# Batch 1's second product as half products in a fused attention and mixer kernel

## The chip, the cores and the metric

The kernel runs on one core of a Trainium2 chip. A core has a matrix engine (TensorE, "PE" in the profile; its weight loads are shown apart as "PEld"), a vector engine (VectorE, "DVE"), an activation engine (ScalarE, "ACT"), a general engine (GpSimd, "POOL") and an engine that mostly issues transfers (SyncE, "SP"). Each works through its own queue of instructions in order, and they meet through semaphores. TensorE's results go to PSUM, eight banks of 512 float32 columns in 128 partitions; a bank that holds a result can be written anew only when another engine has read the result out of it (here called evicting it). The metric is the device time of one execution in microseconds (us), as the median of some runs.

## The reference

Two steps, in float32, on 8 batches of 576 rows.

```python
# attention: q, k, v (8 batches, 8 heads, 576 rows, 64)
phi(x) = concat(relu(x) * cos_w, relu(x) * sin_w)          # 64 -> 128 features
kv  = einsum('bhsf,bhsd->bhfd', phi(k), v);  z = sum_s phi(k)
x   = einsum('bhsf,bhfd->bhsd', phi(q), kv) / (einsum('bhsf,bhf->bhs', phi(q), z) + 1e-6)
# mixer, on x as (8, 576, 512): U (576, 32), V (32, 576), w_ch1 (512, 2048), w_ch2 (2048, 512)
u   = x + (x^T U V)^T
out = u + relu(u @ w_ch1) @ w_ch2
```

Nearly all the arithmetic is in the last line: a *first product* of 512 by 2048 and a *second product* of 2048 by 512 for every row.

## The kernel before

**Rows and tiles.** Of a batch's 576 rows, 512 are four chunks of 128 rows (c = 0 to 3), and 64 are a tail; two batches' tails make one more chunk of 128 (pair pr = 0 to 3). The weights lie in SBUF as bf16 (`w1_bf`, `w2_bf`). Per batch b:

- attention: `q_prep` and `k_prep` (L307 to L327) make the features q_p and k_p from staged float32 loads (qst, kst), 128x512 at a time, on VectorE (L303) or ScalarE (L301); `v_prep` casts v (L130 is the helper that casts on VectorE or GpSimd, L128 the one on ScalarE); SyncE transposes q_p by transfer into q_pT (`qtr_dma`, L386); `kv_unit` (L334) makes kv on TensorE; `x_unit` (L410) and `x_two` (L1151) make x on TensorE, and VectorE normalises it (L407, L408, L427, L1178).
- u: `A_unit` (L447) and `u_mm` (L463) are the low-rank step on TensorE; `u_add` (L476, four a batch) adds x on VectorE into u_bf; `utr_dma` (L510) has SyncE transpose u_bf by transfer into uT, in two halves. `u_tail` (L483) does the same for a pair's tails.
- first product: `g1_main` (L561), 16 units (j) of four 512-column matmuls into a bank of tag "g"; ScalarE evicts each with relu into hid (L580). `g1_tail` (L596) is the same for a pair's tails.
- second product, whole: `g2_part` (L620), for each chunk four parts of four 512-column matmuls, and one eviction on VectorE that adds u (L653) and one store.
- second product, as seven half products: `half_part` (L743). The two chunks n and n + 2 and the two halves of w_ch2 in each direction are the 2x2 blocks of a block product with seven products instead of eight (sums of blocks before, sums of results after). Each half product is eight 256-column matmuls (L772). It needs sums of hid (`hid_sum` L704: four for each n, 128x1024 in bf16 on VectorE, the third and fourth in place) and sums of w_ch2 (`w2_sum` L682: eight halves, 128x1024 in bf16 on VectorE, made once). In the form "with g" the half products alternate with the units of the next batch's first product, in two banks. In the form "alone" they follow each other in three banks, ScalarE copies four of seven results out (L128), VectorE three, and GpSimd makes two additions of 128x512 float32 (L730).

**Order.** It is written out by hand: `slots` is a list of units of TensorE work, recorded one after the other, and `todo` holds what is recorded behind slot n. So every engine's queue is the order in which the slots and what is put behind them are recorded. `PLAN` (L871) gives each batch b its place w, and `attention_plan` (L880) puts the batch's attention at fixed distances from w: for b > 3 q from w - 20 or w - 24, k from w - 13 or w - 14, the transposes of q at w - 12 or w - 14 and on, kv at w and w + 2, x from w + 4, A at w + 14, u_mm at w + 16, the u_adds and their transposes from there; for b = 3 A is at w + 12 and u_mm at w + 14. The last entry of a PLAN row places the loads of the next batch's q, k and v. The slots before the change are:

| slots | unit |
|---|---|
| 0 to 15 | first product of batch 0, with batch 1's attention beside it |
| 16 to 31 | second product of batch 0, four chunks, whole |
| 32 to 47 | first product of batch 1 |
| 48 to 51 | first product of pair 0's tails |
| 52 to 55 | second product of the tails (cc = 4), whole |
| 56 to 71 | second product of batch 1 (cc = 5 to 8), whole |
| 72 to 87 | first product of batch 2 |
| 88 on | for b = 3 to 7: the first product of b, alternating with half products of b - 1 ("with g"), and pair tails |
| last | half products of batch 7 ("alone") and of the last two tails |

Batch 2's attention runs beside slots 30 to 64 (w = 46), batch 3's beside slots 52 to 86 (w = 64). The sums of w_ch2 stand behind slots 56 to 70. Pair 0's stores for chunks 1 to 3 and the tail wait in `late` until slot 92, those of cc = 5 and 6 until slot 65.

**Banks.** `Banks` (L57) hands out banks round robin by tag: g0, g1, g2 for "g", o0 and o1 for "o", two more for "X" and one for "T". `ring` and `turn` (L719) are the list that half products take their banks from.

Of the kernel before, what the change touches and what calls it, by code (L numbers as in the profile page):

```python
# [17 lines left out]
def kernel(  # L18
# [55 lines left out]
    ps = Banks()  # L74
# [543 lines left out]
    late = {}  # L618

    def g2_part(pr, cc, part):  # L620
# [48 lines left out]
            )  # L669

        if pr == 0 and 0 < cc < 7:
            late.setdefault(92 if cc < 5 else 65, []).append(store)
            return
        store()

# [6 lines left out]
    def w2_sum(n, half):  # L682

        a, b = (
            (W2[1], W2[0]), (W2[3], w2_s[0]), (W2[3], W2[1]), (W2[2], w2_s[1])
        )[n]
        js = slice(4 * half, 4 * half + 4)
        V_.tensor_tensor(
            out=w2_s[n][:, js], in0=a[:, js], in1=b[:, js], op=ALU.subtract
        )  # L690
# [169 lines left out]
    ORD = (4, 0, 1, 2, 3)  # L860

    def spare(at):
        if at < 72:
            return ("o", 2) if 32 <= at < 52 else ("g", 3)
        return ("o", 2) if at < 88 else ("s", 1)

    QORD = (4, 0, 1, 2, 3)  # L870
    PLAN = {  # L871
        2: (46, -15, V_, V_, -10, (-5, -4, -4)),
        3: (64, -12, V_, A_, -7, (3, 3, 18)),
        4: (100, (-20, 1, V_, V_), (-13, 2, A_, V_), -12, (-9, -4, -4)),
        5: (127, (-24, 2, A_, A_), (-14, 2, A_, V_), -14, (-8, -4, -4)),
        6: (157, (-24, 2, A_, A_), (-14, 2, A_, V_), -14, (-8, -4, -4)),
        7: (191, (-24, 2, A_, A_), (-14, 2, A_, V_), -14, ()),
    }

    def attention_plan(b):  # L880
# [47 lines left out]


        def two(at):  # L930
            return [T1, ("s", 1)] if at >= 88 else [spare(at)] * 2

        plan.append((w + a_at + 2, lambda: u_mm(b, *two(w + a_at + 2))))
        for j in range(4):
# [49 lines left out]
    T1 = ("T", 1)  # L984
# [219 lines left out]
    def put(at, thunk):  # L1204
        todo.setdefault(at, []).append(thunk)

    def sums(b, n, ats):
        for i, at in enumerate(ats):
            put(at, lambda i=i: hid_sum(b, n, i + 1))
# [4 lines left out]
    def tail_out(pr):  # L1214
        slots.extend(lambda p=p: g2_part(pr, 4, p) for p in range(4))
# [6 lines left out]
    slots += [lambda cc=cc, p=p: g2_part(0, cc, p) for cc, p in early]  # L1222
    slots += [g1(1, j) for j in range(NJ)]
    tail_slots(0)
    slots += [lambda cc=cc, p=p: g2_part(0, cc, p) for cc in range(4, 9) for p in range(4)]
    slots += [g1(2, j) for j in range(NJ)]
    put(len(slots) - 1, lambda: ps.give("g", ("g0", "g1")))
    alone = len(slots)
# [34 lines left out]
    put(at - 2, lambda: tail_store(nc.sync, 3, o_last(1), slice(0, 512)))  # L1263
    put(at - 1, lambda: tail_store(A_, 2, o_last(0), slice(256, 512)))
    for n in range(8):
        put((56, 58, 60, 62, 66, 67, 69, 70)[n], lambda n=n: w2_sum(n // 2, n % 2))
    for j, ts_ in beside.items():
        todo[j] = list(ts_) + todo.get(j, [])

# [10 lines left out]
    for b in range(2, B):  # L1280
        for at, t in attention_plan(b):
            put(at, t)
    for n in (65, 92):
        put(n, lambda n=n: [store() for store in late[n]])
    for i, s in enumerate(slots):
        s()
        for t in todo.get(i, []):
# [31 lines left out]
```

## Time and profile before

| what | value |
|---|---|
| median of 3 runs | 297.0 us (296.45 to 297.48) |
| the profiled execution | 296.4 us, span 294.6 us, granted TensorE clock 1.0 |
| TensorE (PE) busy | 286.1 us, 97% |
| VectorE (DVE) busy | 192.6 us, 65% |
| ScalarE (ACT) busy | 154.7 us, 53% |
| GpSimd (POOL) busy | 51.1 us, 17% |
| one first-product unit, four 512-column matmuls | 0.86 us on the chain |
| one half product, eight 256-column matmuls | 0.87 us on the chain |

The span is the time from the first to the last instruction of the program. In a timeline line the columns are the start and the time taken (us), engine, source line, operation, output tile <- input tiles, shapes and count; in brackets stands the idle time of the engine just before and what ended it. The shown duration of an instruction reaches past the start of the next one on its engine, so what an instruction costs its queue is read from start to start: a sum of w_ch2 lasts 0.68 us and the next instruction starts 0.60 us behind its start. In the chain that ended last, followed back from the last instruction, TensorE has 94% of the span. Lines of waits give the waiting engine, tile and line, the one that it waited for, the total (us), the number of times and the longest.

### The profile page before, as it was taken

The numbers are of one execution on the slowest core, as the hardware profiler recorded it, in microseconds if no ns is written. First come the engines' busy times: TensorE is split into PE (matmuls) and PEld (weight loads), VectorE is DVE, ScalarE is ACT, GpSimd is POOL, SyncE is SP. The second block draws the span as 40 slices with busy tenths as digits, with TensorE's granted clock in tenths as the row PEclk, the third lists the DMA queues.
The fourth block names the chain that finished last, engine by engine and source line by source line (L and its number), as shares of the span: only waits on it lengthen the run. The fifth ranks groups of instructions, "written<-read, shape, count | busy, mean of one in ns | idle before, by whom it ended". The sixth has DMA issues, their size and how long they took to land.

```text
span 294.6 us, 6987 instructions
## 1 busy us (share of the span) xinstructions
PE 286.1 (97%) x2832; PEld 189.4 (64%) x2874; DVE 192.6 (65%) x459; ACT 154.7 (53%) x281; POOL 51.1 (17%) x89
## 2 busy tenths in 40 slices
PE   8999999999999999999989999999999999999995
PEld 6685464447645445676757666766877666668884
DVE  4978656684798887657546794678437755344563
ACT  2956842175880467577826865378743234334310
POOL 8800400012030002500500411031200100000340
PEclk9999999999999999999999999999999999999999
DMA  6999999799998999999989659952900141001013
GB/s 212 330 261 254 261 205 216 173 305 249 280 192 135 283 244 238 234 312 289 232 198 309 162 116 271 289 182 60 246 2 3 73 120 43 36 36 75 2 71 142
DMA packets 90707, 54.05 MB, mean 183 GB/s; under 512 B 58420, under 2 KB 87380, under 8 KB 90676
## 3 DMA queue, kind: packets, MB, share of 16 engines
q1 hardware_dynamic: 84116, 43.85, 62.4%
q0 software_dynamic: 6416, 9.63, 14.0%
q8 instruction: 22, 0.36, 0.5%
q10 hardware_dynamic: 144, 0.13, 0.1%
q14 instruction: 9, 0.07, 0.1%
HBM read 36.86 MB, written 9.44 MB: 157 GB/s over the span
## 4 chain that ended last, share of the span: by engine, by line
PE 94%; DVE 1%; DMA 1%; issue 1%; ACT 1%; SPq 0%; DVEq 0%
PE g_ps L571 36%; PE h_ps L772 27%; PE o_ps L643 10%; PE gt_ps L605 4%; PE w_ps L228 3%; PE kv_ps L342 3%; PE x_ps L417 3%; DMA uT<-u_bf 1%; PE a_ps L440 1%; PE t_ps L372 1%; PE va_ps L470 1%; PE t_ps L360 1%; PE g_ps L588 1%; DVE x_bf L427 0%; PE z_ps L1099 0%
## 5 line engine op out<-in xcount | busy, mean ns | idle before, releaser
L580 ACT ACTIVATE hid<-g_ps 128x512 bf16<-128x512 f32 x128 | 76.2, 597 | 100.9 <-PE g_ps L571 99.4
L571 PE MATMUL g_ps<-uT,w_bf 128*128 128x512 bf16 x474 | 121.1, 379 | 2.3 <-DMA uT<-u_bf 0.9
L571 PEld LDWEIGHTS <-w_bf 128*128 128x128 bf16 x504 | 47.5, 98 | 42.6 <-issue 1.1
L772 PEld LDWEIGHTS <-hid 128*128 128x128 bf16 x480 | 45.4, 98 | 11.8
L730 DVE TENSOR_TENSOR o_sb<-u_bf,h_ps 128x256 f32<-128x256 bf16 x44 | 18.4, 417 | 31.7 <-PE h_ps L772 31.5
L772 PE MATMUL h_ps<-w_bf,hid 128*128 128x256 bf16 x288 | 37.0, 273 | 0.1
L643 PE MATMUL o_ps<-w_bf,hid 128*128 128x512 bf16 x122 | 29.5, 379 | 0.4 <-issue 0.2
L130 POOL CAST v_ext<-vst 128x512 bf16<-128x512 f32 (+1 forms) x26 | 18.3, 729 | 57.3 <-DMA vst<-in_v_dram 46.8
L730 DVE TENSOR_TENSOR o_sb<-o_sb,h_ps 128x256 f32<-128x256 f32 (+1 forms) x36 | 15.5, 432 | 18.7 <-PE h_ps L772 18.5
L772 PE MATMUL h_ps<-w_s,S 128*128 128x256 bf16 x208 | 26.5, 273 | 0.0
L772 PE MATMUL h_ps<-w_s,hid 128*128 128x256 bf16 x192 | 24.9, 272 | 0.0
L830 POOL DMA_DIRECT2D out_dram<-o_sb x16 | 10.0, 625 | 84.4 <-DVE o_sb L730 83.0
L772 PEld LDWEIGHTS <-S 128*128 128x128 bf16 x208 | 19.9, 98 | 5.2
L478 DVE TENSOR_TENSOR u_bf<-x_bf,va_ps 128x512 bf16<-128x512 bf16 x27 | 17.8, 679 | 6.5 <-PE va_ps L470 4.2
L643 PEld LDWEIGHTS <-hid 128*128 128x128 bf16 x128 | 11.6, 98 | 12.5
L427 DVE TENSOR_TENSOR x_bf<-x_ps,rec 128x512 bf16<-128x512 f32 x22 | 15.2, 691 | 0.8
L605 PE MATMUL gt_ps<-uT_tl,w_bf 128*128 128x128 bf16 x256 | 15.6, 219 | 0.0
L605 PEld LDWEIGHTS <-w_bf 128*128 128x128 bf16 x256 | 14.7, 98 | 1.2
L301 ACT ACTIVATE k_p<-kst,cosw 128x512 bf16<-128x512 f32 x20 | 14.2, 713 | 0.4 <-DVE rec L408 0.4
L301 ACT ACTIVATE q_p<-qst,sinw 128x512 bf16<-128x512 f32 x18 | 12.6, 710 | 2.4 <-DMA qst<-in_q_dram 2.4
L303 DVE TENSOR_SCALAR k_p<-kst,sinw 128x512 bf16<-128x512 f32 x23 | 12.7, 554 | 0.0
L342 PEld LDWEIGHTS <-k_p 128*128 128x128 bf16 x240 | 10.5, 97 | 2.6
(170 smaller groups left out, 351.1 us busy)
## 6 DMA issues: line engine op xcount, KB each, us to landing
qst<-in_q_dram SPq DMA_DIRECT2D x14, 512.0 KB, 5.6
kst<-in_k_dram SPq DMA_DIRECT2D x14, 512.0 KB, 8.0
vst<-in_v_dram SPq DMA_DIRECT2D x12, 512.0 KB, 7.9
out_dram<-o_sb POOLq DMA_DIRECT2D x19, 256.0 KB, 3.4
w_bf<-in_moe_w_ch_dram POOLq DMA_DIRECT2D x8, 512.0 KB, 13.1
out_dram<-o_sb SPq DMA_DIRECT2D x16, 256.0 KB, 2.4
qst<-in_q_dram SPq DMA_DIRECT2D x2, 640.0 KB, 8.8
kst<-in_k_dram SPq DMA_DIRECT2D x2, 640.0 KB, 8.3
```

Of the source, the lines that this page charges most:

```text
L130: eng.tensor_copy(out=o, in_=i)
L301: nc.scalar.activation(out=o, in_=i, func=AF.Relu, bias=0.0, scale=w)
L303: eng.tensor_scalar(out=o, in0=i, scalar1=0.0, scalar2=w, op0=ALU.max, op1=ALU.mult)
L342: nc.tensor.matmul(out=acc[:, i, :], lhsT=k_of(b, c, h), rhs=v_tl[:, h, 0:n] if c == 4 and b < 2 else vx[:, c if c < 4 else 4 + b % 2, h, ...
L427: nc.vector.tensor_tensor(out=x_of(b, c, rows).rearrange("p (g i d) -> p g i d", g=2, d=D), in0=view[:, :, :, 0:D], in1=rec[rows].unsqueez ...
L478: nc.vector.tensor_tensor(out=u_bf[b][:, j, :, :], in0=x_bf[b][:, :, ns], in1=va[b][j].rearrange("p (c n) -> p c n", c=4), op=ALU.add,)
L571: nc.tensor.matmul(out=g_ps.rearrange("p (c t) -> p c t", c=4), lhsT=w1_bf[:, d, j * P : j * P + P], rhs=uT[b][:, d, :, :], start=(d == 0) ...
L580: nc.scalar.activation(out=hid[b][:, j, :], in_=g_ps, func=AF.Relu, bias=0.0, scale=1.0)
L605: nc.tensor.matmul(out=g_ps[:, jj, :], lhsT=w1_bf[:, d, j * P : j * P + P], rhs=uT_tl[pr][:, d, :], start=(d == 0), stop=(d == 3),)
L643: nc.tensor.matmul(out=o[:, cols], lhsT=lhs[:, j, c * P : c * P + P], rhs=w2_bf[:, j, cols], start=(j == 0), stop=(j == NJ - 1),)
L730: eng.tensor_tensor(out=o, in0=x, in1=y, op=ALU.add)
L772: nc.tensor.matmul(out=acc, lhsT=lhs[:, j, :], rhs=rhs[:, j, :], start=(j == 0 and at is not None), stop=(j == 7), skip_group_check=at is ...
```

## The change

Batch 1's second product (slots 56 to 71) becomes two times seven half products in the form "alone", in the banks o0, o1 and g2 (slots 56 to 69), and the tags change hands at both ends through `banks_of`: "g" has g0 and g1 alone from slot 55 to slot 69. The sums of batch 1's hid are recorded behind slots 50 to 62, the sums of w_ch2 behind slots 43 to 54 (13 to 18 sooner, and the fourth sum ahead of the third). All that follows moves two slots up. Batches 5, 6 and 7 keep their distance to their own products; batch 4 goes from 100 to 95, three more; batch 3 stays at 64. The stores that waited for slot 92 are issued at slot 65 with nothing else there; batch 1's four stores go through GpSimd's queue.

```diff
         if pr == 0 and 0 < cc < 7:
-            late.setdefault(92 if cc < 5 else 65, []).append(store)
+            late.setdefault(65, []).append(store)
             return
...
     def spare(at):
-        if at < 72:
+        if at < 70:
             return ("o", 2) if 32 <= at < 52 else ("g", 3)
-        return ("o", 2) if at < 88 else ("s", 1)
+        return ("o", 2) if at < 86 else ("s", 1)
...
         2: (46, -15, V_, V_, -10, (-5, -4, -4)),
-        3: (64, -12, V_, A_, -7, (3, 3, 18)),
-        4: (100, (-20, 1, V_, V_), (-13, 2, A_, V_), -12, (-9, -4, -4)),
-        5: (127, (-24, 2, A_, A_), (-14, 2, A_, V_), -14, (-8, -4, -4)),
-        6: (157, (-24, 2, A_, A_), (-14, 2, A_, V_), -14, (-8, -4, -4)),
-        7: (191, (-24, 2, A_, A_), (-14, 2, A_, V_), -14, ()),
+        3: (64, -12, V_, A_, -7, (3, 3, 17)),
+        4: (95, (-20, 1, V_, V_), (-13, 2, A_, V_), -12, (-9, -4, -4)),
+        5: (125, (-24, 2, A_, A_), (-14, 2, A_, V_), -14, (-8, -4, -4)),
+        6: (155, (-24, 2, A_, A_), (-14, 2, A_, V_), -14, (-8, -4, -4)),
+        7: (189, (-24, 2, A_, A_), (-14, 2, A_, V_), -14, ()),
...
-            return [T1, ("s", 1)] if at >= 88 else [spare(at)] * 2
+            return [T1, ("s", 1)] if at >= 86 else [spare(at)] * 2
...
     tail_slots(0)
-    slots += [lambda cc=cc, p=p: g2_part(0, cc, p) for cc in range(4, 9) for p in range(4)]
+    tail_out(0)
+
+    def banks_of(h, g):
+        ring[:] = h
+        turn[0] = 0
+        ps.give("g", g)
+
+    put(len(slots) - 1, lambda: banks_of(["o0", "o1", "g2"], ("g0", "g1")))
+    sums(1, 0, (50, 51, 53))
+    sums(1, 1, (58, 60, 62))
+    for n in range(2):
+        slots.extend(lambda n=n, i7=i7: half_part(1, n, i7, "alone") for i7 in range(7))
+        for i in range(2):
+            put(len(slots) + i, lambda n=n, i=i: half_store(1, n, i))
+    put(len(slots) - 1, lambda: banks_of(["o0", "o1"], ("g0", "g1", "g2")))
     slots += [g1(2, j) for j in range(NJ)]
...
     for n in range(8):
-        put((56, 58, 60, 62, 66, 67, 69, 70)[n], lambda n=n: w2_sum(n // 2, n % 2))
+        put((43, 44, 45, 47, 48, 49, 52, 54)[n], lambda n=n: w2_sum((0, 1, 3, 2)[n // 2], n % 2))
...
-    for n in (65, 92):
-        put(n, lambda n=n: [store() for store in late[n]])
+    put(65, lambda: [store() for store in late[65]])
```

`sums(b, n, ats)` puts the first three hid sums of n behind the slots given; the fourth is recorded by the half product of index 2. In the form "alone" the seven follow in the order 1, 2, 5, 6, 4, 3, 7; product 1 starts the first bank (X), 2 the second (Y), 5 the third (Z), 4 the second again (Q), and 6 and 7 add onto X, 3 onto Z.

## The prediction

> **What bounds the kernel now.** I read the page first: busy time, then the chain that ended last. TensorE is busy for 97% of the span and carries 94% of the chain, at the full granted clock in every slice. VectorE, ScalarE and GpSimd cost time only where TensorE waits for them.
>
> ```profile
> PE 286.1 (97%) x2832; PEld 189.4 (64%) x2874; DVE 192.6 (65%) x459; ACT 154.7 (53%) x281; POOL 51.1 (17%) x89
> PEclk9999999999999999999999999999999999999999
> ```
>
> TensorE's own waits, from the view of waits, are small; the largest is for the transposed input of batch 4's first product, late in the span. So a change gains what it takes from TensorE's queue and loses every wait that it adds there.
>
> ```profile
> PE g_ps L571 <- DMA uT<-u_bf: 0.9, 1, 0.9
> PE x_ps L417 <- DVE x_bf L427: 0.3, 2, 0.2
> ```
>
> Next the stretch of the change, in the busy times by windows: slots 56 to 71 (79.20 to 96.25 us) and batch 2's first product behind them. VectorE is 94% busy in the first stretch (15.99 of 17.05), so it has hardly any slack there.
>
> ```profile
> 79.20:96.25 17.05, 16.89 (x171) 8.89 (x173) 15.99 (x36) 8.19 (x14) 2.23 (x3) 1.00 1.02 175
> 96.25:113.10 16.85, 16.55 (x131) 7.59 (x131) 13.09 (x38) 9.63 (x17) 0.63 (x1) 1.00 1.04 248
> ```
>
> Last the timelines there. TensorE ends the tail's second product and begins slot 56 at 79.22; VectorE reaches the tail's eviction only at 79.97 and ends it at 80.65. Before the change nobody needs that bank soon.
>
> ```profile
> 79.22 1.03 PE L643 MATMUL o_ps<-w_bf,hid 128*128 128x512 bf16 x4
> ...
> 75.33 0.15 DVE L407 TENSOR_SCALAR rec<-x_ps 128x4 f32<-128x4 f32 x1
> 77.44 0.17 DVE L407 TENSOR_SCALAR rec<-x_ps 128x8 f32<-128x8 f32 x1 [0.54 <-PE x_ps L417]
> 79.97 0.68 DVE L653 TENSOR_TENSOR o_sb<-u_tl,o_ps 128x512 f32<-128x512 bf16 x1
> 80.56 0.69 DVE L688 TENSOR_TENSOR w_s<-w_bf 128x1024 bf16<-128x1024 bf16 x1
> ```
>
> And SyncE's queue from batch 3's u to its transposes:
>
> ```profile
> 103.81 0.40 PE L470 MATMUL va_ps<-A_sb,V_bf 32*128 32x128 bf16 x16
> 104.25 1.88 DVE L478 TENSOR_TENSOR u_bf<-x_bf,va_ps 128x512 bf16<-128x512 bf16 x3 [1.86 <-PE va_ps L470]
> 106.84 0.67 DVE L478 TENSOR_TENSOR u_bf<-x_bf,va_ps 128x512 bf16<-128x512 bf16 x1
> 105.56 3.90 SPq L513 DMA_TRANSPOSE uT<-u_bf x2
> DMA to landing us min/median/max: 5.1/5.1/5.1
> ```
>
> **The change, part by part** (the sum stands against the profiled execution: 296.4 us, 294.6 of it span; the median of the runs shown is 297.0).
>
> *Products.* Sixteen slots of four 512-column matmuls at 0.864 (the chain's "0.86 ... x4") are 13.8 us; fourteen of eight 256-column ones at 0.87 are 12.2. TensorE's work falls by **1.6 us**.
>
> *Vector queue ahead of slot 56.* It now also holds eight sums of w_ch2, three of batch 1's hid, all 128x1024 bf16: 0.60 each back to back (80.56 to 81.17; duration 0.69). Seven (six w, the first hid) fall at 68.4 to 74.3, where the queue idles 1.44, 1.93 and 1.61 us: free but for a few tenths that idle time also takes. Four (second and third hid, last two w) stand between the tail's x at 74.31 and the tail's eviction: 2.4 us, less the idle 0.54 at 77.44, so the eviction ends at 80.65 + 1.8 = 82.4. The first half product takes bank o0, in which that tail was summed, so TensorE, ready at 79.22, waits until 82.45. **+3.2 us** (2.9 if a sum overlaps more, 3.5 if it takes its full 0.69). Everything behind it on TensorE waits too; VectorE then idles until slot 56 is done.
>
> *Second bank.* banks_of leaves g only g0 and g1 and gives g2 to the half products. Batch 3's first kv unit (after slot 64) now takes the bank of batch 2's u and waits for its third u_add. Going on from 82.45: VectorE does x (84.8), first eviction, the in-place sum (85.8), a q pair (86.6), S1, a k, A (87.8), S2, a k, the eviction of product 3 (89.1), u_add (89.7). Then the 512-wide addition of product 7 must follow GpSimd's first addition, which follows ScalarE's copy of product 4, which stands behind six k preparations at 0.62 (88.6); GpSimd's takes 1.15, so VectorE ends at 90.5. A hid sum and two u_adds (0.6 to 0.9 each) end at 92.7. TensorE, with nine products (0.87 each), x (0.26), A (0.40) and u_mm (0.44) behind 82.45, is there at 91.4. **+1.3** (0.8 to 2.0).
>
> *Hidden parts.* ScalarE's eight 256-wide copies at 0.38: the first half's stand among k preparations and come 0.6 us or more ahead of their readers; the second half's fall into its idle 9.59 us after 87.7. Bare, they would cost 3.0. GpSimd's four additions (1.15 to 1.71) and four stores (0.63) replace one store; its 14.40 idle before 113.53 hides them. The second half's o2 reuses the first half's o: issue at about 91.8 plus 3.4 to land is 95.2, three slots before product 3 needs the copy at 96.6; 1.2 us of cover, and lost cover would come straight onto TensorE. Three stores leave SyncE at 125.18 (2.85, and the tail's 0.60) and join slot 65.
>
> *Start of g1(2).* The two waits less the saved 1.6 put it at about 98.9 against 96.25. One more x unit of batch 3 lies behind it. Its third slot waits for an x that the late queue gives up about **0.4** late (0 to 0.6).
>
> *Batch 3's transposed u.* Batch 3's plan keeps slots 64 to 85, and g1(3) moves from slot 88 to 86. Before, from the end of u_mm (104.15) to the matmuls that need the second transpose (112.65) are 8.5 us; the transpose is issued at 107.5 and lands 5.1 later, at 112.6: no slack. After, 6.8 us remain. And batch 4's q, three units sooner, is now between A and the u_adds: two pairs ahead of the first, one behind the first, one behind the second; before, one pair stood inside. The q load is itself late: on SyncE it follows batch 2's second transpose (94.2, after the late u_adds, against about 90), q_pT (2.91) and four stores instead of three (0.64 each), so it is issued by 103.0 against 98.9 and lands 5.2 to 6.9 after issue, about 108.0, while u_mm ends at 108.6. Behind it four q operations (1.6) to 109.6, then u_add, pair, u_add (111.6), pair, two u_adds (113.6). With 5.1 to land: 118.7, against 115.3 when TensorE wants it. I take **+3.2**: between 0.2 (q in time, and 2.7 to land, the shortest of such a transpose in 86 to 112 us) and 4.4 (q's load a microsecond later), nearer the upper end because 5.1 is what this very transfer took.
>
> *Batch 4.* Its w goes from 100 to 95 while two slots vanish: three units sooner. v loads go from 82 to 81; kv has 6 us between v's last landing and TensorE at 123.67 now, and three slots (2.6) less plus a later issue use that up: 0 to 1, taken as 0. Its second transpose also leaves SyncE ahead of the second half of batch 5's q_pT (2.48 at 143.96), which it now follows, so the wait of 0.9 goes: **-0.9** (0.6 to 1.0). Batch 5's q_pT in its turn has eleven slots until its x. Batches 5 to 7 keep their places against their products: 0.
>
> Sum: 296.4 - 1.6 + 3.2 + 1.3 + 0.4 + 3.2 - 0.9 = 302.0. The median lies 0.6 above the profiled run; I take half of that: **302.3**.
>
> **Rivals.**
> *A. The vector queue keeps up* (not slower). If the tail's eviction ended by 79.2 and VectorE stayed ahead from there, the 3.2, 1.3 and 0.4 would go. u_mm would end at about 104.2 as now; q's load, with one store more ahead of it, would land at about 104.8 and u's second transpose be issued 5.6 later, at 110.4, against 111.0 when TensorE wants it. With 5.1 to land that is 296.4 - 1.6 + 4.5 - 0.9 = 298.4, with 2.7 it is 296.0: not slower from a landing of 3.1 down. For it: 5.0 us of idle before 74.3, and room for sums there. Against: the eviction is late by 1.4 already, without any new sum ahead of it; VectorE would have to be 3.2 us shorter between 74.3 and 82.4.
> *B. The transpose of batch 3's u is hidden anyway.* With 2.7 to land, the 3.2 falls to 1.0, with q in time too to 0.2: 299.3 to 300.1. For: landings from 2.7 to 5.1 in one stretch. Against: the row of this very transfer.
> *C. The clock.* TensorE's longest idle now is 1.03 us. At its start, from rest, it runs at half speed: 128-column matmuls follow each other every 0.107 us by their starts until 5.5 us into the span and every 0.056 after (26 matmuls start in 4 to 6 us, 40 in 6 to 8), although the granted clock is shown as 1.00 in both.
>
> ```profile
> 4.00:6.00 2.00, 2.00 (x26) 2.00 (x24) 0.46 (x3) 1.15 (x3) 1.88 (x9) 1.00 1.05 341
> 6.00:8.00 2.00, 2.00 (x40) 2.00 (x38) 0.45 (x2) 0.47 (x1) 1.94 (x5) 1.00 1.06 356
> ```
>
> From its first matmul at 1.19 that is 4.3 us. If 3.2 us of rest bring it back, the 4.3 us behind 82.45 do half the work: +2.1, so 304.4. For: the same engine, from rest. Against: no row shows what rest it takes, and the other engines would gain time. [...]
>
> **How the numbers follow.** Forecast 0.60; A 0.12 (a third each faster, within 0.3%, slower); B 0.16; C 0.12. About 0.3%, 0.9 us, is what a measurement of this kernel can tell from no change. Slower: 0.60 + 0.16 + 0.12 + 0.04 = 0.92, faster 0.04, same 0.04. The low ends of all terms (-1.6 + 2.9 + 0.8 + 0 + 0.2 - 1.0) give 298.0 with the median's 0.3, the high ends (-1.6 + 3.5 + 2.0 + 0.6 + 4.4 + 1.0 - 0.6) 306.0. All at once are rare, so the range is **299.0 to 305.0**: it takes in B and C and leaves out A.
>
> **What would show it.** In TensorE's waits: one of about 3.2 us for o_sb (the tail's eviction) ahead of the first half product; one of 1.3 for u_bf ahead of a kv unit; one of some 3 us for uT at g1(3) and none at g1(4). VectorE's tail eviction begins near 81.7, g1(2) near 98.9, and half products behind the gap take 0.87 from start to start. The forecast is wrong if the eviction begins before 80 or if uT of batch 3 lands within 3 us of its issue; C is right if those half products take 1.7.

## The result, and the profile after

The kernel is slower: 308.0 us median (304.2 to 311.9) against 296.7, a ratio of 1.034 with a 95% interval of 1.024 to 1.043. The median is that of all four executions; the ratio leaves out the one of 311.9 us, which counts as slow. Six more executions, later, beside the kernel before, gave 310.6 us and 1.044 (1.039 to 1.048). The forecast was 302.3 us with a range of 299.0 to 305.0: right in direction, too low in size. All eleven executions of the changed kernel have a median of 308.7; their fastest is the one profiled first, at 304.2 us (span 302.5).

The page of that execution, its busy line and the clock in 40 slices:

```profile
PE 286.6 (95%) x2883; PEld 195.5 (65%) x2922; DVE 197.9 (65%) x469; ACT 157.1 (52%) x289; POOL 57.5 (19%) x96
PEclk9999999999997999999999999999999999999999
```

TensorE is busy as long as before (286.6 against 286.1 us) though its work fell by 1.6: the clock row, which was 9 throughout before, has a 7. TensorE's waits of 0.5 us and more, where the view of before had one of 0.9 behind the opening:

```profile
PE h_ps L772 <- DVE o_sb L653: 3.1, 1, 3.1
PE g_ps L571 <- DMA uT<-u_bf: 2.1, 2, 1.4
PE kv_ps L342 <- DVE u_bf L478: 2.1, 1, 2.1
...
PE kv_ps L342 <- POOL v_ext L130: 0.7, 1, 0.7
PE g_ps L571 <- DVE x_bf L1175: 0.5, 1, 0.5
```

All the waits that were forecast are there (their sizes further down), and two that were not: one for batch 4's v, and, as the second of the two for uT, the one at batch 4's first product, which the forecast had as gone. The timeline at the first and the second wait:

```profile
79.61 0.68 DVE L688 TENSOR_TENSOR w_s<-w_bf 128x1024 bf16<-128x1024 bf16 x1
...
81.69 0.68 DVE L653 TENSOR_TENSOR o_sb<-u_tl,o_ps 128x512 f32<-128x512 bf16 x1
...
82.42 1.03 PE L772 MATMUL h_ps<-w_bf,hid 128*128 128x256 bf16 x8 [3.07 <-DVE o_sb L653]
...
89.73 1.91 PE L772 MATMUL h_ps<-w_bf,hid 128*128 128x256 bf16 x16
93.72 0.28 PE L342 MATMUL kv_ps<-v_ext,k_p 128*128 128x65 bf16 x4 [2.08 <-DVE u_bf L478]
...
94.32 3.11 PE L772 MATMUL h_ps<-w_s,S 128*128 128x256 bf16 x16
```

The tail's eviction begins at 81.69 (forecast: near 81.7), and the first half product 3.24 us after TensorE is ready (forecast 3.2). (The idle time in brackets counts from the shown end of the last matmul. Four 512-column matmuls start 0.216 us apart and show 1.03 us together, so the shown end lies 0.17 past the moment at which the next could start. Waits and rests in the text count from that moment: 3.24 for the 3.07 shown.) But the sixteen matmuls at 94.32 take 3.11 us, where the sixteen at 89.73 take 1.91. The busy times by windows, with the granted clock in the column behind the five engines:

```profile
77.80:81.21 3.41, 1.55 (x14) 0.74 (x13) 3.24 (x11) 3.30 (x6) 0.00 (x0) 1.00 1.15 278
81.21:84.62 3.41, 2.19 (x26) 1.99 (x26) 1.93 (x6) 1.10 (x3) 0.61 (x1) 1.00 1.03 243
91.45:94.86 3.41, 1.33 (x27) 1.12 (x26) 3.41 (x7) 0.00 (x0) 1.65 (x3) 1.00 0.36 127
94.86:98.26 3.40, 3.40 (x32) 2.71 (x31) 0.59 (x2) 0.77 (x2) 0.00 (x0) 0.50 1.32 133
```

The clock is 0.50 from 94.86 to 98.26, for 3.40 us, and shown as 1.00 in the rest of the span. So TensorE does 1.7 us less work there, and the shown mean clock is 0.994 (one such stretch in 302.5 us is 0.0056 of it). That is rival C, but not where it was looked for: the half products right behind the wait of 3.2 us take 0.87 us from start to start, not the 1.7 that the prediction named as C's sign, and the fall comes behind the shorter wait of 2.25. The other executions of the changed kernel show mean clocks of 0.989 (twice), 0.982 or 0.983 (five times), 0.978 (twice) and 0.976, by their size two to four stretches each. (The count is rough: a fall behind the last matmul, as at 299.2 us in the profile with a rest of 3.5 us further down, takes nothing from TensorE and can be in the mean too.) Their times go with it: 304.2 us at 0.994, 307 to 308 at 0.989, 307 to 311 at 0.983, 311 to 312 at 0.978 and below. That is some 2.4 us for each stretch, more than the 1.7 that a stretch takes from TensorE, so the clock is not all that varies.

### The profile page after: what moved, and what is told of

The parts are those of the page before. It is cut to its first block, busy times and chain, and to the rows that moved or that the text cites. A ratio compares the mean times of both kernels' runs of the same rounds, so it can differ in the third digit from the quotient of the medians.

```text
span 302.5 us, 7109 instructions
## 1 busy us (share of the span) xinstructions
PE 286.6 (95%) x2883; PEld 195.5 (65%) x2922; DVE 197.9 (65%) x469; ACT 157.1 (52%) x289; POOL 57.5 (19%) x96
## 4 chain that ended last, share of the span: by engine, by line
PE 79%; DMA 8%; DVE 5%; SPq 3%; issue 2%; ACT 1%; POOL 1%; DVEq 0%; POOLq 0%; ACTq 0%
PE g_ps L571 29%; PE h_ps L772 26%; PE gt_ps L605 5%; PE o_ps L643 4%; PE w_ps L228 3%; PE kv_ps L342 3%; DMA qst<-in_q_dram 2%; DMA q_tlT<-q_tl 2%; PE x_ps L417 2%; DMA vst<-in_v_dram 2%; DVE u_bf L478 1%; DVE q_p L303 1%; DMA uT<-u_bf 1%; POOL v_ext L130 1%; PE a_ps L440 1%
## 5 line engine op out<-in xcount | busy, mean ns | idle before, releaser
L580 ACT ACTIVATE hid<-g_ps 128x512 bf16<-128x512 f32 x128 | 76.2, 597 | 97.6 <-PE g_ps L571 95.9
L772 PEld LDWEIGHTS <-hid 128*128 128x128 bf16 x560 | 52.4, 98 | 14.8 <-issue 3.4
L772 PE MATMUL h_ps<-w_bf,hid 128*128 128x256 bf16 x336 | 43.1, 273 | 3.2 <-DVE o_sb L653 3.1
L730 DVE TENSOR_TENSOR o_sb<-u_bf,h_ps 128x256 f32<-128x256 bf16 x48 | 20.0, 416 | 29.5 <-PE h_ps L772 29.3
L772 PE MATMUL h_ps<-w_s,S 128*128 128x256 bf16 x240 | 31.5, 280 | 0.0
L772 PE MATMUL h_ps<-w_s,hid 128*128 128x256 bf16 x224 | 29.0, 273 | 0.0
L830 POOL DMA_DIRECT2D out_dram<-o_sb x20 | 12.6, 628 | 86.1 <-DVE o_sb L730 83.9
L772 PEld LDWEIGHTS <-S 128*128 128x128 bf16 x240 | 23.4, 100 | 5.6
L605 PEld LDWEIGHTS <-w_bf 128*128 128x128 bf16 x256 | 14.7, 98 | 1.2
L643 PE MATMUL o_ps<-w_bf,hid 128*128 128x512 bf16 x61 | 14.6, 379 | 0.3 <-issue 0.2
L342 PE MATMUL kv_ps<-v_ext,k_p 128*128 128x65 bf16 (+1 forms) x240 | 11.7, 196 | 2.8 <-DVE u_bf L478 2.1
L407 DVE TENSOR_SCALAR rec<-x_ps 128x8 f32<-128x8 f32 (+2 forms) x39 | 6.3, 163 | 11.3 <-PE x_ps L417 9.3
```

The source lines that it names most:

```text
L342: nc.tensor.matmul(out=acc[:, i, :], lhsT=k_of(b, c, h), rhs=v_tl[:, h, 0:n] if c == 4 and b < 2 else vx[:, c if c < 4 else 4 + b % 2, h, ...
L580: nc.scalar.activation(out=hid[b][:, j, :], in_=g_ps, func=AF.Relu, bias=0.0, scale=1.0)
L605: nc.tensor.matmul(out=g_ps[:, jj, :], lhsT=w1_bf[:, d, j * P : j * P + P], rhs=uT_tl[pr][:, d, :], start=(d == 0), stop=(d == 3),)
L643: nc.tensor.matmul(out=o[:, cols], lhsT=lhs[:, j, c * P : c * P + P], rhs=w2_bf[:, j, cols], start=(j == 0), stop=(j == NJ - 1),)
L730: eng.tensor_tensor(out=o, in0=x, in1=y, op=ALU.add)
L772: nc.tensor.matmul(out=acc, lhsT=lhs[:, j, :], rhs=rhs[:, j, :], start=(j == 0 and at is not None), stop=(j == 7), skip_group_check=at is ...
```

## The experiments

Theory C' was that the waits sum up about as forecast and that the clock makes the rest. Rival D was that the excess lies in waits that vary, for transfers above all, and the clock is a side matter. The kernel before, run beside each group, had medians of 296.5, 296.5, 296.7, 296.8, 296.9 and 296.5 us.

### Filling the waits, and a rest by itself

Dummy matmuls keep TensorE at work in the first wait, the second, or both; a fourth kernel puts a rest into the kernel before.

```
+ def fill(n):                       # n 512-column matmuls of weights into bank X
+     x_w = ps.tile([P, 512], FP32, tag="X", ...)
+ put(len(slots) - 1, lambda: fill(12))    # first wait
+ put(64, lambda: fill(9))                 # second wait
```

> The changed kernel with 12 dummy 512-column matmuls (2.6 us) in TensorE's wait ahead of the first half product and 9 (1.9 us) in its wait ahead of batch 3's first kv unit, into a bank that nobody needs then. The waits for VectorE stay as they are, only TensorE is not at rest in them. Theory C (the two rests take TensorE's clock to half speed, for a stretch that differs from run to run; the shown granted clocks of 0.994, 0.983, 0.982 and 0.978 times the spans leave 300.1 to 303.2 us of span): granted clock 1.000, span 300 to 301.5, median 302 to 303 us, and the runs within 1.5 us of each other. Rival D (the time above the forecast is waits that differ from run to run, and the clock is a side matter): median 306 to 309 as before, spread as before.

> Only the first wait (3.2 us at 79.2) is filled with 12 dummy matmuls; the second (2.2 us at 91.5) stays a rest. In the profiled execution of the changed kernel the matmuls came at full speed behind the first wait and at half speed only some 3 us behind the second. If the second rest alone brings the clock down, this is 304 to 308 us with a granted clock below 0.995; if it takes the long rest of 3.2 us, this is 302 to 303 with a clock of 1.000. Rival D: 306 to 309 whatever the clock.

> Only the second wait (2.2 us at 91.5) is filled, with 9 dummy matmuls; the first (3.2 us) stays a rest. If the rest of 3.2 us brings the clock down, 304 to 308 us with a clock below 0.995; if the second does, 302 to 303 with a clock of 1.000. Rival D: 306 to 309 whatever the clock.

The fourth (`hold` steps the bank of tag "o" back by one, `late_sum` is a sum of 128x1024 into an unused tile):

```
+ put(55, hold)
+ for _ in range(3): put(54, late_sum)
```

> The kernel before with a rest of about 3.2 us put into TensorE at 79.2 and nothing else changed: slot 56 takes the bank in which the tail was summed, and three needless sums of 0.6 us stand ahead of the tail's eviction on VectorE (written to a tile that is not yet in use). The rest alone makes 296.7 + 3.2 = 299.9 us (299 to 300.5). Theory C: more than that, by 2 to 6 us (302 to 306), with a granted clock below 0.995. Rival D: 299 to 300.5 and a clock of 1.000.

| kernel | median us | mean granted clock of the runs |
|---|---|---|
| both waits filled | 308.6 (307.5 to 309.0) | 1.000, 0.997, 0.994, 0.993, 1.000 |
| first filled | 307.2 (305.7 to 311.5) | 0.994, 0.993, 0.989, 0.993, 0.994, 0.983 |
| second filled | 305.8 (305.0 to 308.6) | 0.994, 0.989, 0.986, 1.000, 0.981, 1.000 |
| before, with a rest of 3.5 us | 301.4 (299.9 to 302.5) | 0.992, 0.997, 0.994, 0.988, 0.994, 0.994 |

The last row is clean: 296.5 and 3.4 more of waiting (3.53, less the 0.1 between two units) make 299.9; measured are 1.5 us more. Its profile has one stretch of 0.50 among the matmuls, at 84.14 to 87.55 us, right behind the rest. The times of its runs follow their clocks: 299.9 us at 0.997, so the rest alone, 301.1 to 301.5 at 0.994, which is one stretch, and 302.5 at 0.988. So a rest can have a price beyond its length.

Each of the two waits of the changed kernel had a stretch of 0.50 behind it in the profile in which the other was filled: with the first filled it stands behind the second (95.9 to 99.3 us), with the second filled behind the first (82.5 to 85.9).

The first three rows contradict theory C' in its simple form. With both waits filled the clock is back in three of five runs and in the profile, and the time isn't; with the second filled the two runs at 1.000 take 305.1 and 305.6 us and the one profiled, at 0.994, 305.0. One reason is a flaw of the filling: bank X holds a quarter of batch 2's u, so the second filling itself waited 1.6 us for a u_add and then took 1.9, where the wait had been 2.25. That is some 1.5 us lost, and the two kernels with this filling are to be read for their clock alone. Another reason is in their profiles: the waits for transposed u and for v behind 118 us come to 6.2 us in the kernel with both filled (0.7, 1.6, 1.0, 0.5, 1.1, 1.3; the view puts the first of them down to ScalarE's eviction), against 3.4 in the changed kernel's first profile. These 2.8 us more and the 1.5 are most of what is to be explained: the two profiles' spans differ by 4.0 us, and by 4.6 once the clock of the changed kernel's (1.7) and the longer opening of the filled one's (1.1) are allowed for. So rival D has its part, and the next kernels take the waits away.

### Taking the causes of the waits away, one after the other

```
- put((43, 44, 45, 47, 48, 49, 52, 54)[n], lambda n=n: w2_sum(...))
+ put((24, 24, 25, 37, 41, 43, 45, 47)[n], lambda n=n: w2_sum(...))
- banks_of(["o0", "o1", "g2"], ("g0", "g1"));  sums(1, 0, (50, 51, 53))
+ banks_of(["o1", "g2", "o0"], ("g0", "g1"));  sums(1, 0, (48, 49, 50))
```

> The changed kernel without the cause of its first wait: five of the eight sums of w_ch2 go to slots 24 to 41, where VectorE waits for transfers and for TensorE, the other three to 43, 45 and 47, the first three sums of hid to 48 to 50, and the first half product takes bank o1 in place of the bank of the tail. Theory (waits for VectorE, each rest with its price in clock): the wait of 3.2 us is gone, TensorE comes to batch 3's kv unit 3.2 us sooner but VectorE's u_adds only some 2.4 us sooner (four sums of 0.6), so that wait becomes 2.5 to 3.2 us; median 303 to 306 us, the granted clock still below 1.000 in most runs. Rival D (the waits for transposed u and for loads behind 100 us set the end, so nothing is gained ahead of them): 306 to 309.

```
+ kv_at = ("T", 1) if b == 3 else spare(w)     # and kv_unit(b, 0, *kv_at, ...)
```

> As the kernel with early sums, and batch 3's first kv unit takes bank T, which is free then, in place of the bank that waits for batch 2's u_adds. Theory: neither of the two rests is left, the granted clock is 1.000 in nearly all runs and the runs lie within 1.5 us of each other; some of the wait comes back as short waits for k features or the next bank (0.5 to 1.5 us); median 298.5 to 301.5. Rival D: at most 1 us below the kernel with early sums alone, and the waits for transposed u grow by what is gained.

```
- 3: (64, -12, V_, A_, -7, (3, 3, 17)),    4: (95, ...
+ 3: (64, -12, V_, A_, -7, (3, 3, 18)),    4: (98, ...
```

> As the one before, and batch 4's attention at slot 98, its distance to its own product as in the kernel before (q's features then come behind batch 3's u_adds). Theory: batch 3's transposed u is no longer late (wait of 0 to 0.5 in place of 1.6), the kv wait of 0.9 goes, the wait at batch 4's own product stays near 0.9; median 296 to 299. Rival: the three units cost nothing on TensorE, and this equals the one before within 0.5 us.

The last step alone, in the changed kernel:

> The changed kernel with nothing but batch 4's attention put back to slot 98. Theory: the two waits for VectorE stay (3.2 and 2.2 us); the waits at batch 3's product (1.6) and at batch 4's kv unit (0.9) go, the one at batch 4's product (0.9) stays or grows by 0.3: 2 us below the changed kernel's median of 308, so 304.5 to 307, with the clock below 0.995 as there. Rival: no different from the changed kernel, 307 to 309.

| kernel | median us | clock of the runs |
|---|---|---|
| sums early | 304.9 (303.9 to 305.9) | 0.994, 0.994, 0.989 (four) |
| ... and kv in bank T | 303.8 (302.4 to 305.0) | 0.994 (two), 0.988 (three), 0.982 |
| ... and batch 4 at 98 | 298.0 (296.8 to 298.6) | 1.000 (ten), 0.997 (two) |
| batch 4 at 98 alone | 302.4 (301.8 to 304.9) | 0.994 (four), 0.993, 0.986 |

Each wait goes where its cause is taken away: no wait ahead of the first half product in the first row (the one at the kv unit is 2.1), none at the kv unit in the second. (The first row moves the sums and changes the bank at once; which of the two would have sufficed is not shown.) But the second row gains 1.1 us where 3 to 6 had been expected. And the place of batch 4, which the forecast had as a gain of 0.9 at its own product and part of a loss at batch 3's, is worth 5.8 us in one pair (303.8 to 298.0) and some 6 in the other (308.7 to 302.4), where 2 had been expected. In the second pair the waits of the profiles account for some 2.5 us. The clocks account for more: four of the six runs are at 0.994, one stretch, where the changed kernel has mostly three. The second row's VectorE timeline shows what batch 4's early place does, at batch 3's u_adds:

```profile
106.61 0.28 DVE L130 CAST A_sb<-a_ps 128x128 bf16<-128x128 f32 x1
110.52 0.49 DVE L303 TENSOR_SCALAR q_p<-qst,cosw 128x512 bf16<-128x512 f32 x1 [3.63 <-issue]
...
112.11 0.68 DVE L478 TENSOR_TENSOR u_bf<-x_bf,va_ps 128x512 bf16<-128x512 bf16 x1
```

VectorE idles 3.6 us ahead of batch 4's q, with batch 3's u_adds queued behind it. (The line names no releaser; in the changed kernel the same operation waits 1.7 us and the line names q's load.) There TensorE's two waits had hidden the larger part; without them it shows, and TensorE waits 4.8 us in five pieces around the tail's u and the first product of batch 3. And there is no single rest over 1.6 us among these pieces, yet the clock fell in all six runs. The windows of the second row's profile:

```profile
111.48:114.89 3.41, 2.52 (x13) 1.04 (x12) 3.41 (x9) 3.06 (x6) 0.00 (x0) 1.00 0.08 28
114.89:118.30 3.41, 1.07 (x8) 0.42 (x8) 3.41 (x11) 0.15 (x1) 0.00 (x0) 1.00 0.66 150
118.30:121.72 3.42, 2.72 (x7) 0.99 (x7) 1.04 (x3) 1.21 (x2) 0.60 (x1) 0.50 0.68 155
```

In the second of these windows TensorE has 2.84 us of rest, in four pieces of 0.5 to 0.9 (the line shows 2.34 idle, and each of three pieces that begin in the window is 0.17 longer), and the 3.42 us behind it are at a clock of 0.50.

### The clock in that row of short waits, batch 4's q alone, and the changed kernel again

Here the filling stands in bank T, which is free, and replaces rest alone (8 matmuls behind slot 84, 4 behind 85, 6 between the two halves of batch 3's first unit, `(b, j, d) == (3, 0, 2)` in `g1_main`):

> The kernel with early sums and the kv unit in bank T, and 18 dummy 512-column matmuls (3.9 us) in bank T, which is free there, in TensorE's row of short waits around batch 3's u tail and first product (0.6, 1.3, 0.5, 0.7 and 1.6 us between 113.6 and 119.0, behind which the shown clock was 0.58 for 4 us): 8 ahead of the tail's u, 4 ahead of the product, 6 between its two halves. What TensorE waits for is not changed. Theory (no wait there is over 1.6 us, but a stretch of 5.4 us in which TensorE works for a fifth brings the clock to half): granted clock 0.997 to 1.000, median 301 to 302.5, 1.5 to 3 us below that kernel's 303.8. Rival (the clock falls for another reason, or TensorE's lost speed is made up by shorter waits behind it): clock 0.988 and 303 to 305.

```
- 4: (95, (-20, 1, V_, V_), ...          # q of batch 4: slots 75 to 79
+ 4: (95, (-14, 1, V_, V_), ...          # slots 81 to 85; the changed kernel otherwise
```

> The changed kernel with only the preparation of batch 4's q five units later, behind batch 3's u_adds on VectorE; k, v, kv and everything else of batch 4 stay at 95. Theory E (of the three units, it is the q preparations between A and the u_adds that cost: they wait for q's late load, and batch 3's u waits behind them): the wait at batch 3's product goes from 1.6 to at most 0.3 us, the ones at batch 4's kv unit and product (0.9 and 0.9) stay; the clock as with batch 4 at 98 (0.994); median 303 to 305. Rival F (the later v load, kv and transposes of batch 4 cost as much): 306 to 308.

```
- 4: (98, (-20, 1, V_, V_), ...          # in the 298.0 us kernel
+ 4: (98, (-16, 1, V_, V_), ...
```

> As the kernel with early sums, kv in bank T and batch 4 at 98 (298.0 us), and batch 4's q prepared four units later, behind batch 3's u_adds, which it still separates there. Theory E: the waits of 0.8 and 1.0 for batch 3's transposed u go to 0 to 0.4, clock 1.000, median 296.3 to 297.2, so no measurable difference from the kernel before or a little faster. Rival: the wait moves to batch 4's q transposes and the time stays at 298.

> The changed kernel itself, unchanged, beside the others on the same chip. Theory C': 306 to 309 with granted clocks from 0.978 to 0.994, and each 0.006 of clock goes with about 1 to 2 us of span. Rival D: the times spread with the clock unchanged.

The filled kernel's windows, at the same places:

```profile
111.48:114.89 3.41, 3.41 (x18) 1.50 (x16) 3.41 (x9) 2.38 (x5) 0.00 (x0) 1.00 0.09 26
114.89:118.30 3.41, 3.32 (x23) 1.40 (x22) 3.41 (x10) 0.60 (x1) 0.00 (x0) 1.00 0.66 148
118.30:121.72 3.42, 3.42 (x23) 2.10 (x22) 1.40 (x4) 2.49 (x5) 0.60 (x1) 1.00 0.83 203
```

With TensorE at work the fall is gone, in all six runs (1.000 four times, 0.998 twice, against 0.982 to 0.994), so it is the rest there that brings it. The time is 303.3 (302.0 to 304.8), only 0.5 below. Some of the 1.7 us that TensorE has back returns as waiting: behind 122 us this profile has 2.7 us of waits (batch 4's kv unit and batch 5's first product), the unfilled one 1.7. So here a fall was worth little at the end, where in the kernel before it was worth 1.5 us.

Batch 4's q by itself, six units later (the expectation says five), gives 303.6 (301.9 to 305.9): some 5 to 7 us of the changed kernel's excess. Theory E holds for batch 3's u: in the profile no wait for it is left. It does not hold for the waits that it had as staying: at batch 4's kv unit 0.35 us are left of 0.9, and at its first product 2.5 stand where 0.9 did. Clocks 0.994 (three), 0.992, 0.989, 0.987. In the 298.0 us kernel the same step gave nothing (298.0; ratio to before 1.003, 1.000 to 1.005): there the u_adds ended 3.2 us sooner and the transposed u still landed at 114 to 115 us.

The changed kernel again: 310.6 us, clocks 0.978, 0.983 (three), 0.976, 0.989. In its profile (span 309.3) the 0.50 stretches lie at 16.64 to 23.46, 98.56 to 101.97 and 125.86 to 129.27; the first, two windows long, is in the opening that the change doesn't touch, where TensorE waited 1.7 us for batch 0's v at 15.4.

### How much rest, what sets the landing, and three tries to come below the kernel before

```
+ for _ in range(0): put(54, late_sum)     # rest of 1.5 us; and range(6): 5.7 us
```

The window theory of the next three expectations is the author's reading of the profiles so far: stretches of 3.41 us at 0.50, whole steps of 3.41 from each other (24 and 8 steps from 16.64 to 98.56 and on to 125.86, in the profile just named), and pieces of 3.41 us with 2.02 us of rest without a fall behind them and with 2.13 with one (the last section has all).

> The kernel before with slot 56 in the tail's bank and no needless sums: a rest of about 1.5 us at 79.2. Window theory (the clock goes to half for one window of 3.41 us, cost 1.7 us, when TensorE rests for more than about 2.1 us inside one of the windows of 3.41 us that run freely): the clock never falls there, so 296.6 + 1.45 = 298.0 us (297.5 to 298.5), granted clock 0.997 to 1.000. Rival (every rest costs clock in proportion): 298.7 and a clock near 0.997 in all runs.

> The kernel before with a rest of about 5.2 us at 79.2 (six needless sums ahead of the tail's eviction). Window theory: always at least one window with over 2.1 us of rest, in a third of the runs two; a window at half speed that falls into the rest itself costs nothing: 296.6 + 5.2 + 0.5 to 1.7 = 302.3 to 303.8 us, granted clock 0.989 to 0.995. Rival (cost in proportion to the rest, by the 1.5 us that 3.4 us of rest cost): 296.6 + 5.2 + 2.3 = 304.1 or more.

> The changed kernel again, for the places of its half-speed windows. Window theory: each stretch at 0.50 is 3.41 us long or a multiple, the distances between their starts are multiples of 3.41 us, and each stands behind a window with over 2.1 us of rest; 307 to 311 us with a clock near 0.983. Rival: stretches of other lengths, or ones behind which no such rest lies.

The rest of 1.5 us gave 298.0 us (297.4 to 298.7) with 0.998 to 1.000, so nothing beyond its length: 296.8 + 1.4 are 298.2. The rest of 5.7 us, half a microsecond longer than meant, gave 304.4 (303.6 to 305.0) with 0.987 to 0.989: 296.8 + 5.6 + 2.0. A price in proportion, from the 1.5 us that 3.5 us of rest cost, would have been 0.6 and 2.4. The short rest speaks against it. The long one does not decide: 2.0 lies between 2.4 and the 1.7 that the window theory allows at most, and by their clocks all five runs had two windows at half speed, where the theory expected that in a third. The windows of the long one:

```profile
78.41:81.82 3.41, 1.40 (x14) 0.65 (x12) 3.27 (x6) 2.88 (x5) 0.00 (x0) 1.00 1.13 277
81.82:85.23 3.41, 0.00 (x0) 0.00 (x0) 3.24 (x10) 2.97 (x6) 0.61 (x1) 0.50 1.30 242
85.23:88.65 3.42, 3.30 (x15) 1.45 (x15) 1.56 (x5) 3.42 (x7) 1.17 (x2) 0.50 0.10 14
```

Two windows at 0.50, the first of them spent wholly in the rest and so free. And the changed kernel once more, 307.4 us at 0.989:

```profile
81.65:85.06 3.41, 0.85 (x8) 0.76 (x8) 2.37 (x8) 1.19 (x2) 0.61 (x1) 1.00 1.30 289
85.06:88.47 3.41, 3.41 (x24) 2.51 (x23) 2.05 (x6) 2.94 (x5) 1.17 (x2) 0.50 0.76 98
119.19:122.60 3.41, 1.07 (x8) 0.42 (x8) 3.41 (x10) 0.19 (x1) 0.00 (x0) 1.00 0.68 154
122.60:126.01 3.41, 2.85 (x8) 1.14 (x8) 0.88 (x2) 1.30 (x3) 0.60 (x1) 0.50 0.70 163
```

This time the fall is behind the first wait, with 2.56 us of it inside one window, and behind the waits for batch 3's u (2.84). From 85.06 to 122.60 are 37.54 us, 11 times 3.41; in the profile of 309.3 us the falls are 24 and 8 times 3.41 apart, in that of q alone 19 times. So in these three profiles the falls keep whole steps of 3.41 us from each other, across stretches of full clock too, and where a wait falls in such a step differs from execution to execution: behind the first wait the clock falls here, and not in the other two profiles of the changed kernel.

Last, three variants of the 298.0 us kernel with q late. In it, the loads of batch 4's k stand on SyncE right ahead of batch 3's transposes, which take 5.0 us on the queue and land late. Batch 0's late stores go from slot 65 to 60, ahead of batch 2's transposes:

> As the kernel with early sums, kv in bank T, batch 4 at 98 and its q late (298.0 us), and batch 0's four late stores recorded behind slot 60 in place of 65: SyncE issues them while it idles (86.5 to 91), ahead of batch 2's transposes, and the loads of batch 4's q and k some 3 us sooner. Theory G (batch 3's transposes land late because q and k of batch 4, 4 MB issued in the 5 us ahead of them, are still in the transfer engines): the waits of 1.35 and 0.5 at batch 3's product go to 0 to 0.6 in sum, median 296.3 to 297.2, not measurably slower than the kernel before. Rival: 298 as before (the transposes take 5 us whatever is ahead of them), or slower, where the stores delay batch 2's transposes.

Or k is loaded behind the transposes (`3: (..., (3, 17, 18))` and `4: (98, (-16, 1, V_, V_), (-9, 1, A_, V_), ...`):

> As the kernel with early sums, kv in bank T, batch 4 at 98 and its q late (298.0 us), and the loads of batch 4's k issued behind batch 3's transposes in place of ahead of them, its k features prepared from slot 89 on in place of 85. Theory G: with 2 MB less ahead of them the transposes land in 2.6 to 3.5 us, the waits of 1.35 and 0.5 at batch 3's product go to 0 to 0.5, batch 2's waits are not touched; median 296.3 to 297.3, unless batch 4's kv unit then waits for k or v (0 to 1.5). Rival (the transposes take 5 us whatever is ahead of them): 298.

In that kernel the loads of batch 5's v came ahead of the last of batch 4's v casts, so 128 of batch 4's rows were computed with batch 5's v. With that order mended (`(-9, -4, -2)` as batch 4's last entry):

> As the run before it, with batch 5's v loaded two units later, behind the last of batch 4's v casts (in that run the last cast stood behind that load, so it computed with batch 5's v and TensorE waited 18.8 us for it). Theory G: the transposes of batch 3's u land within 3.5 us of their issue, no wait at batch 3's product, 0 to 1 us at batch 4's kv unit, granted clock 0.997 to 1.000; median 296.3 to 297.5. Rival: batch 4's k and v, 2 us later, make its kv unit wait for what was gained: 298.

The moved stores gave 298.4 us (296.5 to 300.4): batch 3's wait was gone, and waits of 1.0 and 0.9 stood at batch 2's first product and 1.1 at a half product behind 123 us. The mixed-up order gave 317.6 us, with one wait of 18.8 us for v and six windows at 0.50. The mended one gave 298.5 us (297.1 to 300.5; 1.008, 1.005 to 1.010). SyncE's queue in it, and then the same two transposes in the kernel that it varies:

```profile
107.98 2.62 SPq L513 DMA_TRANSPOSE uT<-u_bf  x2
```

```profile
107.87 5.03 SPq L513 DMA_TRANSPOSE uT<-u_bf  x2
```

Without k's 1.2 MB ahead of them (8 heads of 576 by 64 in float32; the expectations have k at 2 MB, and q with k at 4) they pass in 2.6 us instead of 5.0, and TensorE's wait for batch 3's u is gone (1.8 before). Theory G holds for the landing, but none of it reached the end: no variant came below the kernel before, 298 against 296.5 to 296.8 beside them. Their profiles say where most of the gain went (spans of 295.6 to 297.0 us, clocks of 0.998 to 1.000). TensorE's waits of over 0.25 us behind the opening come to 4.2 to 5.7 us, against 2.3 in the kernel before: 1.9 to 3.4 more, which takes back the 1.6 us of the products. Whether that is all of the 1.5 us in the medians is open.

## Why the prediction was wrong

Three profiles of the changed kernel, by the prediction's own terms (us on TensorE, waits counted as above; the products at the forecast's figure; span of before 294.6):

| term | forecast | 302.5 | 309.3 | 305.6 |
|---|---|---|---|---|
| Products | -1.6 | -1.6 | -1.6 | -1.6 |
| Vector queue ahead of slot 56 | +3.2 | 3.2 | 3.2 | 3.2 |
| Second bank | +1.3 | 2.3 | 2.3 | 1.2 |
| Start of g1(2), x late | +0.4 | 0.7 | 0.7 | 0.7 |
| Batch 3's transposed u (with the tail's u) | +3.2 | 1.6 | 2.3 | 4.1 |
| Batch 4: kv unit, and own product against 1.0 before | -0.9 | +0.7 | +0.6 | -0.7 |
| clock behind the opening | 0 | 1.7 | 3.4 | 3.4 |
| opening (up to slot 0) | 0 | 0.1 | 4.4 | 1.9 |
| sum | 5.6 | 8.7 | 15.3 | 12.2 |
| span less 294.6 | | 7.9 | 14.7 | 11.0 |

(The sums are 0.6 to 1.2 too high. Small waits of before that these profiles do not have, 0.3 to 1.0 us, are not in them, and the clock's row counts each stretch in full.)

- **The step that failed** is rival C and how the numbers followed from it. "The clock" stood beside the sum, at a chance of 0.12 and with one fall of +2.1, so the sum had nothing for it. Every wait that the forecast itself put in was a chance for a fall; the range had room for one, and the runs have one to four. In the three profiles the clock behind the opening takes 1.7, 3.4 and 3.4 us from TensorE, and the opening (two windows at 0.50 included, in one) adds 0.1 to 4.4. Less both, the spans are 300.7, 301.5 and 300.3, and with the 1.8 us around a span 302.1 to 303.3. So the sum of the waits came out at the forecast, and that is partly luck: the terms below miss by up to 1.6 us, in both directions. The subtraction is a reckoning and no run: how much a fall costs at the end was 1.5 us in the kernel before, and 0.5 or nothing where later waits took it up. What part of the median's 5.7 us above the forecast is the clock therefore stays open.
- *Products* and *Vector queue*: right, to 0.1 us, the place of the eviction too. *Hidden parts*: right in the changed kernel. The tight cover named there (the copy into o2 behind the store of the first half) ran out in the faster variants, where TensorE waits 0.3 to 0.9 us for that copy.
- *Second bank*: right mechanism, mis-sized where it is 2.3. VectorE's k operation ahead of the u_adds took 1.38 us instead of 0.48. The rows are in the last section.
- *Start of g1(2)*: the wait for x came to 0.7, just outside 0 to 0.6, and g1(2) began at about 101.2 us instead of 98.9, behind the longer second wait and the fall.
- *Batch 3's transposed u*: 1.6 to 4.1, inside 0.2 to 4.4, but by two misses that cancel in part. The second transpose landed 2.8 us after its issue in all three profiles, not 5.1; by the prediction's own sign (within 3 us) this step was wrong. So 5.1 was no fixed price of "this very transfer". It was probably what the loads ahead of it left: with k's loads right ahead the second transpose landed in 4.5 us, with k's loads behind it in 2.8 (the 298.0 us kernel with q late, and its last variant). On the other side q's load landed at about 111.4 instead of 108.0, and the transpose was issued at 117.2 instead of 113.6. The rows of the first profile are these; TensorE, later too, wanted the transpose at 118.5 (forecast 115.3). With q prepared later the wait is gone, so it is q's lateness that the wait comes from. What the early q costs in all, 5 to 7 us by the run of q alone, is more than any term of the forecast had for it.

```profile
111.53 0.48 DVE L303 TENSOR_SCALAR q_p<-qst,cosw 128x512 bf16<-128x512 f32 x1 [1.69 <-DMA qst<-in_q_dram]
...
115.22 3.23 SPq L513 DMA_TRANSPOSE uT<-u_bf  x2
...
DMA to landing us min/median/max: 2.8/2.8/2.8
```

- *Batch 4*: wrong in sign in two of three. The wait at its own product stayed at 0.9, 1.6 and 0.3, and the cover at kv, "0 to 1, taken as 0", was 0.9 in one.
- Rival A: the runs speak against it, the vector queue did not keep up (3.24 in all three). Rival B is right in its condition, a landing of 2.7 to 2.8, and wrong in its outcome: the wait was 1.6 to 4.1 us, not 1.0 or less, as u itself came later.

What makes the opening vary is open, but the change does not touch it. ScalarE evicts the first unit of batch 0's first product at 24.4 us in the profile of before, and at 24.5, 28.9 and 26.3 in these. The code up to there is the same in all kernels of this document, and in the other 16 profiles the eviction starts at 24.6 to 26.5; in the kernel before with a rest added, at 24.8, 25.0 and 25.9. So some 2 us of it come and go whatever the kernel; the 4.4 us stand in one profile alone.

## What to carry to other kernels

On a kernel whose matrix engine is full, price a new wait twice: its length, and the clock behind it. Here a rest of 3.5 us cost 1.5 us more than its length, one of 1.5 us nothing more, and each stretch at 0.50 took up to 1.7 us from TensorE. Put the sum of such chances into the range. Look for short waits that stand close together, and not only for the longest: here four pieces of 0.5 to 0.9 us, 2.84 in sum, had such a stretch behind them. And when work is moved sooner, ask of each queue that it joins when its input lands: here VectorE stood still for a load (1.7 us in the changed kernel's first profile) while the work that TensorE needed next was queued behind it.

## What the runs showed of the hardware

**The stretches at 0.50.** In the twelve profiles in which the clock falls inside the kernel it is shown as 1.00 or 0.50, the 0.50 in stretches of 3.40 to 3.42 us or whole multiples. From the start of such a stretch each profile was cut into windows of 3.41 us, both ways. Of the windows behind 24 us, all those with 2.13 us of rest or more (2.13, 2.18, 2.25, 2.27, 2.29, 2.32 three times and up to 3.41) were followed by one at 0.50, and all those with 2.02 or less (2.02, 1.85, 1.82, 1.74, 1.73) were not. The eight profiles without such a fall have no window with over 1.9 us of rest between 24 us and the last matmul. The first profile has both: the wait of 3.24 us falls on two windows as 2.02 and 1.22, with no stretch at 0.50 behind either, the wait of 2.25 falls inside one, with a stretch behind it. In the opening a window with 1.2 us of shown rest was followed by 0.50 once, in the changed kernel's profile of 309.3 us (13.23 to 16.64 us); what was different there is not shown. So a wait of 2.13 us (the 302.1 us profile of the kernel with the sums early), or four pieces of 2.84 in sum, had a fall behind it, and one of 3.24 had none, in two of the changed kernel's three profiles.

**VectorE's k operation beside GpSimd's addition.** The k operation of the second bank's term, with GpSimd's addition, in the changed kernel:

```profile
88.58 1.29 POOL L730 TENSOR_TENSOR o_sb<-o_sb,u_bf 128x512 f32<-128x512 f32 x1 [2.20 <-ACT o_sb L128]
88.77 1.38 DVE L303 TENSOR_SCALAR k_p<-kst,sinw 128x512 bf16<-128x512 f32 x1
```

and with batch 4 at 98 alone:

```profile
90.20 0.48 DVE L303 TENSOR_SCALAR k_p<-kst,sinw 128x512 bf16<-128x512 f32 x1
90.38 1.32 POOL L730 TENSOR_TENSOR o_sb<-o_sb,u_bf 128x512 f32<-128x512 f32 x1 [4.04 <-ACT o_sb L128]
```

Where it begins inside the addition it ends 0.28 us behind it (89.87 and 90.15; the same in four more profiles, within 0.01), and where it begins first it takes 0.48. The wait at the kv unit is 2.25 to 2.32 us in the first case and 1.16 to 1.30 in the second.
